# A gated-decay attention, Sinkhorn MoE and bilinear kernel: expert 0 and the gate's logits by 512 tokens, and a first list planned with DMA issue

## The chip, the cores and the metric

One core of one Trainium2 chip. The metric is the device time in microseconds of one execution; the lower the better. PE is TensorE, DVE is VectorE, ACT is ScalarE, POOL is GpSimd, SP is SyncE, which here issues most of the DMAs.

## What is computed

Three layers over 4 x 768 = 3072 tokens, all float32:

```
state = f[t,:,None] * state + k[t] (x) v[t]; y[t] = q[t] @ state     # 4 batches, 8 heads of 48; f = sigmoid(f_logit)
P = exp(y @ w_gate - max); 8 rounds: rows to sum 1, columns to sum 1, times N/E    # 8 experts
x2 = sum over e of P[:, e] * (relu(y @ w1[e]) @ w2[e])              # 384 -> 1024 -> 384
out = ((x2 @ w_a) * (x2 @ w_b)) @ w_out                             # 384 -> 1536 -> 384
```

Products run in a reduced format: every operand is split into a high and a low part, and each product is three matmuls (high x high, high x low, low x high).

## The kernel before, in words

The kernel adds operations to a `Plan`, each with an engine, a cost, the keys it reads and writes and a priority. A scheduler turns the plan into one order for all engines, and the program is issued in that order: each engine works off its own instructions in it strictly one after the other. There are two plans, so two lists.

**The first list** holds the attention, in 24 steps of 128 tokens (`attention`, L624). A step is a chain: transposes of f, q and k (L654), decay factors on ACT and DVE, four groups of small matmuls with masked copies between them (m0 at L697, m8 at L709, m16 at L741, m32 at L752), a transpose of the keys (L763), the state's update (L782), y (L810, L816), and six small DMAs that put y into a tile `xf` with 384 features over partitions. Each buffer of a step exists twice, so two steps are under way at a time, and step s + 2 reuses the buffers of step s: its `q3` (L701) waits until the DMAs of step s have read it.

Beside it, as filler for PE, the first list computes most of expert 0 (`expert0`, L862): x of a block of `EB` = 256 tokens times w1, seven tiles of 128 hidden units with nine matmuls of 256 columns each (L516, the *front*), relu and the split of h on ACT and POOL (L875, L878, L880), then h times w2 (the *down* product). Tokens 0 to 1023 take the down product with tokens over partitions, 384 columns a matmul (L528); blocks in `TURNED` groups (tokens 1024 to 3071) take it with features over partitions, 256 columns a matmul (L539). There are 12 blocks; blocks 0 to 9 and the front of block 10 are in the first list, the down product of block 10 and block 11 in the second. The gate's logits are made per step: six matmuls with x as the stationary side and 16 or 8 columns (`logits`, L854), and a reduce on DVE. Before the first block has its x, PE is kept running by spare matmuls that compute nothing (L917; the plan holds 400, and the list takes as many as fit before the first filler).

The order of the first list comes from `Plan.order` (L132): it keeps a time for each engine, fixed gaps between engines and one delay `LATE` for a DMA; a filler is preferred on PE while a running balance `due`, fed by `SHARE` of the attention's PE time, is not negative. Weights of expert 0 are loaded into two `raw` tiles (`add_piece`, L494) and split into high and low on ACT and POOL (L484, L486) as soon as they land.

**The second list** starts with what is left of expert 0 and the last logits, then the Sinkhorn rounds (`sinkhorn`, L929; each round is one small matmul, L966, between two groups of DVE operations), and then seven experts and the bilinear layer in jobs: a front of 15 products of three matmuls with 512 columns (L1258), whose sums of products run over ACT and DVE (L1539), and backs of 384 or 512 columns (L528, L539). Its first five x pairs `xs` and the weights of its first two jobs (`w1t`) are made ready in the first list (`x_take`, `w1_load`, `w1_split`). Its order comes from `Plan.timed` (L239), which runs `Plan.listed` (L270) 60 times with changed priorities and keeps the best; `listed` already reckons with DMA issue, queue and lanes.

## Time and profile before

| | us |
|---|---|
| runs, lowest / median / highest of 3 | 2155.32 / 2157.52 / 2165.69 |
| the profiled execution's own time | 2153.39 |
| its span, first to last instruction | 2151.6 |
| PE busy (99% of the span) | 2134.3 |
| DVE / POOL / ACT busy | 1720.0 / 1184.4 / 940.9 |

A busy time of PE counts matmuls whose modelled ends overlap the next one's start; the cost of a matmul in a stream is therefore read below from the start of one row to the start of the next. The first list's PE work runs from 0 to about 414 us of the span, the second list from there to the end.

### The profile page before, as it was taken

To read this page: it belongs to the slowest core of one execution; us is meant where nothing else is said; L and a number is where in the kernel's file an instruction comes from. 1 tells how busy PE (TensorE), PEld (TensorE's weight loads), DVE (VectorE), ACT (ScalarE), POOL (GpSimd) and SP (SyncE) were. 2 spreads that over 40 slices of the span, in tenths; PEclk is the share of its full clock that TensorE was granted. 3 is DMA by queue.
4 is the path that set the end of the run, shared out by engine and by line. 5 is a ranking of instruction groups with operands and counts; after the bars stand their busy time and mean duration, and the time that the engine had idled before them with its cause. 6 is when DMAs were issued, how large, how long until landed. Compare 5 with 4: busy or idle time off the path is not lost.

```text
span 2151.6 us, 41006 instructions
## 1 busy us (share of the span) xinstructions
PE 2134.3 (99%) x15371; PEld 1869.3 (87%) x15371; DVE 1720.0 (80%) x2882; ACT 940.9 (44%) x1761; POOL 1184.4 (55%) x1106
## 2 busy tenths in 40 slices
PE   8999999999999999999999999999999999999999
PEld 8999999989989999988888888888888888888888
DVE  7878888377878777698888986899998887866656
ACT  3544454454444445444444444444343445533331
POOL 2212121268877666477787767755545688535322
PEclk9999999999999999999999999999999999999999
DMA  6546644356675567865657678777665766878552
GB/s 133 116 106 165 166 112 98 109 203 241 235 254 196 185 223 267 279 227 194 219 179 232 198 273 279 243 255 247 226 199 174 239 218 228 302 232 283 172 173 74
DMA packets 340951, 438.66 MB, mean 204 GB/s; under 512 B 148024, under 2 KB 224656, under 8 KB 337296
## 3 DMA queue, kind: packets, MB, share of 16 engines
q1 hardware_dynamic: 326016, 422.40, 60.9%
q10 hardware_dynamic: 14736, 13.64, 1.9%
q8 instruction: 121, 1.98, 0.4%
q14 instruction: 78, 0.64, 0.1%
HBM read 295.58 MB, written 135.64 MB: 200 GB/s over the span
## 4 chain that ended last, share of the span: by engine, by line
PE 96%; DVE 3%; DMA 1%; issue 0%; ACT 0%; SPq 0%; DVEq 0%
PE pG L1258 28%; PE pR L539 21%; PE pR L528 18%; PE pF L1258 10%; PE pM L516 4%; PE pM L539 2%; PE pT L654 1%; PE pM L528 1%; PE pA L697 1%; PE pM L917 1%; PE pO L810 1%; PE pA L709 1%; PE pA L741 1%; PE pO L816 1%; PE pO L782 1%; DVE z L1539 1%
## 5 line engine op out<-in xcount | busy, mean ns | idle before, releaser
L539 PE MATMUL pR<-er 128*128 128x512 f32 (+1 forms) x2178 | 537.8, 383 | 0.0
L1258 PE MATMUL pG<-xs,w 128*128 128x512 f32 x1701 | 469.0, 392 | 3.6 <-DVE z L1539 3.0
L539 PEld LDWEIGHTS pR<-er 128*128 128x128 f32 x2178 | 401.1, 188 | 80.5
L528 PE MATMUL pR<-er 128*128 128x384 f32 x2232 | 433.8, 336 | 0.0
L1539 ACT ACTIVATE z<-pG 128x512 f32<-128x512 f32 x397 | 237.2, 598 | 437.5 <-PE pG L1258 370.5
L528 PEld LDWEIGHTS pR<-er 128*128 128x128 f32 x2232 | 397.6, 188 | 23.9
L1258 PEld LDWEIGHTS pG<-xs,w 128*128 128x128 f32 x1701 | 315.9, 188 | 64.3 <-DVE z L1539 3.2
L1539 POOL TENSOR_TENSOR er<-z,er 128x512 fp32r<-128x512 f32 x177 | 246.5, 1400 | 195.9 <-ACT er L1539 135.2
L1539 POOL TENSOR_TENSOR acc<-acc,tmp 128x512 f32<-128x512 f32 x168 | 232.4, 1390 | 173.3 <-DVE tmp L1539 172.3
L1539 ACT ACTIVATE er<-z 128x512 fp32r<-128x512 f32 x353 | 217.6, 628 | 212.4 <-PE pR L539 123.8
L1258 PE MATMUL pG<-er,w 128*128 128x512 f32 x972 | 276.5, 393 | 2.8 <-DVE z L1539 2.6
L1539 DVE TENSOR_TENSOR z<-pF,z 128x512 f32<-128x512 f32 x268 | 182.2, 684 | 64.4 <-PE pF L1258 42.8
L880 POOL TENSOR_TENSOR er<-l,er 128x256 fp32r<-128x256 f32 x84 | 74.6, 891 | 282.3 <-ACT l L878 234.5
L1258 PEld LDWEIGHTS pG<-er,w 128*128 128x128 f32 x972 | 180.9, 188 | 36.5 <-DVE z L1539 4.7
L1539 DVE TENSOR_TENSOR z<-z,pG 128x512 f32<-128x512 f32 x206 | 140.4, 682 | 63.5 <-PE pG L1258 61.9
L1539 POOL TENSOR_TENSOR stage<-stage 128x128 f32<-128x128 f32 x325 | 168.7, 551 | 19.8 <-DMA stage<-in_moe_w_dram 18.2
L1539 DVE SCALAR_TENSOR_TENSOR er<-z,er 128x512 fp32r<-128x512 f32 x150 | 146.6, 986 | 7.4 <-ACT er L1539 7.1
L1539 DVE SCALAR_TENSOR_TENSOR acc<-pR,prob,acc 128x384 f32<-128x384 f32 x168 | 100.5, 611 | 63.0 <-PE pR L528 60.6
L486 POOL TENSOR_TENSOR er<-raw,er 128x384 fp32r<-128x384 f32 (+1 forms) x82 | 94.4, 1159 | 101.8 <-ACT er L484 96.8
L1539 POOL TENSOR_TENSOR w<-stage,w 128x512 fp32r<-128x512 f32 (+2 forms) x75 | 125.0, 1677 | 38.4 <-ACT w L1539 33.5
L1258 PE MATMUL pF<-er,w 128*128 128x512 f32 x486 | 138.8, 394 | 0.0
L1258 PE MATMUL pF<-xs,w 128*128 128x512 f32 x486 | 136.8, 391 | 0.0
(283 smaller groups left out, 3227.0 us busy)
## 6 DMA issues: line engine op xcount, KB each, us to landing
er<-w2d SPq DMA_DIRECT2D x138, 384.0 KB, 4.4
wfmoe<-w SPq DMA_DIRECT2D x19, 1920.0 KB, 7.2
w<-wfmoe SPq DMA_DIRECT2D x38, 768.0 KB, 5.3
w2d<-er SPq DMA_DIRECT2D x69, 384.0 KB, 4.2
w<-wfmoe SPq DMA_DIRECT2D x38, 640.0 KB, 5.6
w<-wfmoe SPq DMA_DIRECT2D x38, 512.0 KB, 4.8
wfout<-w SPq DMA_DIRECT2D x8, 1920.0 KB, 7.7
raw<-in_moe_w_dram SPq DMA_DIRECT2D x64, 192.0 KB, 2.6
```

The lines of the kernel that those rows point to most:

```text
L486: plan.add(prio + 1, "POOL", S_COST[0] + m * S_COST[1], [gk, key], [key], lambda: nc.gpsimd.tensor_tensor(out=lj, in0=got, in1=f32(hj), op ...
L516: nc.tensor.matmul(out=ps, lhsT=a[:, kk, fs], rhs=b[:, kk, :], start=(i == 0), stop=(i == 3 * KD - 1),)
L528: nc.tensor.matmul(out=ps, lhsT=a[:, off:off + 128], rhs=b, start=(start and i == 0), stop=(stop and i == n - 1))
L539: nc.tensor.matmul(out=ps, lhsT=a[:, d * 128:d * 128 + 128], rhs=b, start=(start and i == 0), stop=(stop and i == n - 1))
L654: nc.tensor.transpose(ps[0:R, p * 128:p * 128 + 128], src[:, p * 128:p * 128 + R], ident)
L697: nc.tensor.matmul(out=A0[o:o + 64, w, :], lhsT=pct(bk)[r, g, :], rhs=pct(bq)[r, g, :])
L709: nc.tensor.matmul(out=A1[o:o + 56, 0, w, :].rearrange("j (b e) -> j b e", e=8), lhsT=pct(k3)[r, g, 0:56], rhs=qv[r, g, :, 1, :])
L741: nc.tensor.matmul(out=A1[o:o + 48, 1, w, :].rearrange("j (b e) -> j b e", e=16), lhsT=pct(k3)[r, g, 0:48], rhs=qv[r, g, :, 1, :])
L782: nc.tensor.matmul(out=ps[64 * hd:64 * hd + m, p * D:(p + 1) * D], lhsT=kn[64 * c:64 * c + 64, p * R + 64 * hd:p * R + 64 * hd + m], rhs=b ...
L880: op(POOL, .76, [f"hh{ft}", kf], [f"hl{ft}"], lambda hh=hh, hl=hl, hf=hf: nc.gpsimd.tensor_tensor(out=hl, in0=hf, in1=f32(hh), op=ALU.subt ...
L1258: nc.tensor.matmul(out=ps, lhsT=a[:, slot], rhs=b, start=(new and i == 0), stop=(i == 2), skip_group_check=not new)
L1539: fn()
```

## The change

Expert 0 goes by eight blocks instead of 12 (`E0_BLOCKS`): four of 256 tokens (tokens 0 to 1023, as before) and four of 512 (tokens 1024 to 3071), whose fronts are tiles of nine matmuls with 512 columns and whose down products have 512 columns too. The wide blocks need room: x of blocks 4 and 6 lies in the first three `xs` pairs of the second list, the low part of h in the `w1t` tile of its second job. So the x pairs 0 to 2 can be made only after block 6's front, and the second job's weights are now loaded and split at the start of the second list, behind block 7. Blocks 0 to 5 and the front of block 6 are in the first list; the down product of block 6 and all of block 7 (three times 63 matmuls of 512 columns) in the second.

The logits of blocks 0 to 6 are made turned (`logits_turned`): the gate's weights are the stationary side, 256 or 512 tokens the columns, six matmuls a block; ACT copies the 16 rows out and one transpose for each 128 tokens brings them back. Block 7 keeps the old way. Pieces of expert 0's weights go through five staging tiles instead of two, and their splits wait for a key of attention (`W_AFTER`): the first for the first masked copy of step 0, the others for the x of steps 0 and 1.

The first list now comes from `Plan.first`, a timed list with ranks: costs fitted to this stage (`FIRST`), the shared port of DVE and POOL (operations marked `DVE+`, which many of attention's now are), a cost of changing between attention and filler on PE (`turn`), SP's time to issue each DMA, eight DMAs under way and one queue for their transfers. `SHARE` is 0.3 instead of 0.6. The second list starts from the times at which the first leaves each engine (`late`).

```diff
+    def first(self, share, sooner):
...
+        while any(todo.values()):
+            at, eng = min((max(free.get(eng, 0.0), min(held(n) for n in ns)), eng) for eng, ns in todo.items() if ns)
...
+            turn = due >= 0.0
+            n = min((n for n in todo[eng] if held(n) <= at + 1e-9), key=lambda n: (eng == "PE" and self.ops[n][6] != turn, prio[n]))
...
+            _, _, cost, _, _, late, fill = self.ops[n]
+            cost = self.FIRST[eng].get(round(cost, 3), cost)
+            other = held_by.get(eng) if ready[n] < free.get(eng, 0.0) - 1e-6 else None
+            if n in self.shared and port - .03 > at:
+                at, other = port - .03, on_port
+            if eng == "PE":
+                at = max(at, free[eng] + self.turn(kind, last, self.kind[n]))
+                kind, last, ever = self.kind[n], cost, ever or fill
+                due = max(min(due + (-cost if fill else share * cost), self.MOST), -self.DEBT)
+            count, each = sizes[n]
+            end = at
+            for i in range(count):
+                end = max(end, lanes[landed % self.LANES]) + cost / count
+                queue = max(end + 1.9, queue) + each
+                lanes[landed % self.LANES] = queue + .06
+                landed += 1
+            cost = end - at if count else cost
...
-    SHARE = 0.6
-    LATE = 4.0
-    S_COST, X_COST = (.1, .0026), .9
+    SHARE = 0.3
+    LATE = 2.5
...
+    E0_BLOCKS = [(256, "p"), (256, "q"), (256, "p"), (256, "q"), (512, "r"), (512, "pq"), (512, "r"), (512, "pq")]
+    E0_LEFT = 1.5
+    LG_OLD = 7
+    W1_ON = "DVE"
+    MANY = 2
+    W_BY, W_READS, WG_AFTER = "SP", [], "bk0"
+    W_AFTER = ["X0"], ["st0"], ["st1"]
...
+    ring_of = raw_of + stage_of
...
-        x = count["raw"] % len(raws)
+        x = count["raw"] % len(ring_of)
         count["raw"] += 1
-        raw, rk = raws[x][:, :m], f"raw{x}"
...
+        plan.add(prio, by, cost * len(parts) if by == "SP" else 1.17, reads, rk, get, late)
+        split_ops(plan, prio + 9, raw, [*rk, *after], hj, lj, key, m)
...
+    x_p = er_take(2 * KD * HALF)
+    h_p = er_take(2 * NF0 * HALF)
...
+    x_q = er_take(2 * KD * HALF)
+    x_r = x_all[:, 0:3].rearrange("p a b -> p (a b)")
+    w_r = w1t[1].rearrange("p a b c -> p (a b c)")
...
+    def h_of(b, ft):
+        n = e0_blocks[b][1]
+        lo = area("w", n * ft, n) if n == TB else area("h", n * (NF0 + ft), n)
+        return area("h", n * ft, n), lo
...
+    def logits_turned(plan, b, prio, nm, bufs):
+
+        t0, n, _ = e0_blocks[b]
+        (xH, kH), (xL, kL) = x_tiles(b)
+        m, rk, rt = n // 128, f"raw{b % 2}", raws[b % 2]
+        kl, psl = take(nm, bufs)
+        for i, (x, keys) in enumerate(((xH, kH), (xL, kL))):
+            def lg(i=i, x=x):
+                for kk in range(KD):
+                    nc.tensor.matmul(out=psl[0:2 * E, :n], lhsT=wgs[:, kk], rhs=x[:, kk], start=(i == kk == 0), stop=(i == 1 and kk == KD - 1))
+
+            plan.add(prio, PE, .681 if n == TB else .36, [*keys, *holds(b, True), "wgs"], [kl], lg, kind=5)
+        plan.add(prio, ACT, .6 if n == TB else .37, [kl], [rk], lambda: nc.scalar.activation(
+            out=rt[0:2 * E, :n], in_=psl[0:2 * E, :n], func=AF.Copy))
+
+        def turn():
+            for j in range(m):
+                nc.tensor.transpose(psl[:, 2 * E * j:2 * E * (j + 1)], rt[0:2 * E, 128 * j:128 * j + 128], ident[0:2 * E, 0:2 * E])
+
+        plan.add(prio, PE, .06 * m, [rk], [kl], turn)
+        plan.add(prio, DVE, .16, [kl], [f"lg{t0 // 128 + j}" for j in range(m)], lambda: nc.vector.tensor_reduce(
+            out=logit[:, t0 // 128:t0 // 128 + m, :], in_=psl[:, :2 * E * m].rearrange("p (s two e) -> p s e two", two=2, e=E),
+            axis=AX.X, op=ALU.add))
...
+            for kk in [None]:
+                op(PE, 2.04 if n == TB else 1.08, [*kH, *kL, *holds(b, True), *(wi if kk is None else wi[kk:kk + 1])], [km, "E0i"],
+                   partial(gemm_f, psm[:, :n], w_e0[ft // FT][0], ft % FT, (xH, xL), kk), 0.0, fill)
+            big = n == TB
+            op(ACT, .6 if big else .37, [km], kh, partial(nc.scalar.activation, out=hh, in_=psm[:, :n], func=AF.Relu))
+            hf, kf = b_l[0][:, :n], "l0"
+            op(ACT, .6 if big else .37, [km], [kf], partial(nc.scalar.activation, out=hf, in_=psm[:, :n], func=AF.Relu))
+            op(POOL, 1.29 if big else .76, [*kh, kf], kl, partial(
+                nc.gpsimd.tensor_tensor, out=hl, in0=hf, in1=f32(hh), op=ALU.subtract))
...
+        many = MANY if turned and n == TB else 2
+        for d in range(KD if turned else n // 128):
+            km, psm = take(nm, bufs)
+            cost = .53 if not turned else .681 if n == TB else .36
+            to = psm[:, :n if turned else DM]
+            for f0 in range(0, NF0, many):
+                fs = slice(f0, min(f0 + many, NF0))
+                op(PE, cost * (fs.stop - f0), [k for x in hk[fs] for k in x] + wk[fs] + holds(b), [km, "E0o"], partial(
+                    gemm_d if turned else gemm_t, to, hs[fs], ws[fs], d if turned else d * 128, f0 == 0, fs.stop == NF0), 0.0, fill)
...
+    def e0_weights(u, outs, after):
...
     for i in range(NSTEP):
+        if i == 0 and not W_AFTER[0]:
+            e0_weights(0, False, [])
         attention(i)
+        if i == 0 and W_AFTER[0]:
+            e0_weights(0, False, W_AFTER[0])
+        if i == 1:
+            for u, outs, after in ((1, False, W_AFTER[1]), (0, True, W_AFTER[2]), (1, True, W_AFTER[2])):
+                e0_weights(u, outs, after)
         if i == 0:
...
-        if i:
-            logits(plan, i - 1, 1000 * i + 500, "O", p_O)
-        if i % 2 == 1 and i + 1 < NSTEP:
-            expert0(plan, i // 2, 1000 * (i + 1), "M", p_M, True, 0 if i + 3 > NSTEP - 1 else None)
+        if i and block_of[i - 1] >= LG_OLD:
+            logits(plan, i - 1, 1000 * i + 500, "O", p_O, True)
+        b = block_of[i]
+        if b < LG_OLD and block_of[i + 1] != b:
+            logits_turned(plan, b, 1000 * (i + 1), "O", p_O)
+        if b < len(e0_blocks) - E0_LEFT and block_of[min(i + 1, NSTEP - 1)] != b:
+            expert0(plan, b, 1000 * (i + 1), "M", p_M, True, 0 if b + 1 > len(e0_blocks) - E0_LEFT else None)
...
-    for n in range(2):
+    for n in range(1 if e0_blocks[-1][1] == TB else 2):
         w1_load(plan, 1000 * (15 + 3 * n), n, [f"st{14 + 3 * n}"])
         w1_split(plan, 1000 * (15 + 3 * n) + 600, n, DVE)
     with tc.manual_schedule():
-        for fn in plan.order(SHARE):
+        plan.ranks()
+        for fn in plan.timed(partial(plan.first, SHARE), 1, 0):
             fn()
...
-    plan.add(-9000, "clock", 8.0, [], [f"x{(NSTEP - 1) % 4}"], lambda: None)
-    expert0(plan, NSTEP // 2 - 2, -8000, "R", p_R[:2], False, 1)
+    plan.add(-9000, "clock", max(x_at, 0.0), [], x_of(NSTEP - 1)[1], lambda: None)
+    left = len(e0_blocks) - E0_LEFT
+    for x, b in enumerate(b for b in range(len(e0_blocks) - 1) if b + 1 > left):
+        expert0(plan, b, -8000 + 700 * x, "R", p_R[:2], False, 1 if b < left else None)
     logits(plan, NSTEP - 1, -4000, "R", p_R[:2])
-    expert0(plan, NSTEP // 2 - 1, E0_AT, "R", p_R[:2], False)
+    expert0(plan, len(e0_blocks) - 1, E0_AT, "R", p_R[:2], False)
     guard += ["E0i", "E0o", f"lg{NSTEP - 1}"]
+    if e0_blocks[-1][1] == TB:
+        w1_load(plan, -2000, 1)
+        w1_split(plan, -1000, 1, W1_ON)
...
-        for fn in plan.timed(.08, 0.0, 60, 200):
+        for fn in plan.timed(partial(plan.listed, .08, 0.0), 60, 200):
```

How the order changes on the engines. Over both programs the first list's PE order holds 693 front matmuls of 256 columns, 378 down of 256 and 168 of 384 before, in 136 stretches (66, 46 and 24) between other work; in the change 252 front of 256, 168 down of 384, 189 front and 126 down of 512, in 90 stretches (22, 28, 18 and 22). Spare matmuls fall from 193 to 185, and the 48 transposes, three m0 and so on that precede the first filler are the same.

PE in the first list, a place in a block of tokens from 1024 on; before (`pM` is expert 0's bank, `pA` and `pT` attention's; m16 is the 48x32 group, m32 the 32x32 one):

```order
L539 MATMUL pM_167<-er 128x256 x12
L516 MATMUL pM_166<-er 128x256 x9
L752 MATMUL pA_165<-q_137,k_139 32x32 x16
L539 MATMUL pM_167<-er 128x256 x3
L654 MATMUL pT_160<-ident,nat_f_117 112x128 x4
L697 MATMUL pA_164<-bq_132,bk_134 64x64 x16
L763 MATMUL pO_162<-ident,k_139 128x112 x4
L516 MATMUL pM_167<-er 128x256 x9
```

And in the change (L642 is the front, L869, L901, L857 and L912 are m8, m16, m0 and m32):

```order
L869 MATMUL pA_161<-q_132,k_134 56x32 x16
L642 MATMUL pM_163<-xs,er 128x512 x9
L901 MATMUL pA_161<-q_132,k_134 48x32 x16
L857 MATMUL pA_160<-bq_129,bk_131 64x64 x16
L814 MATMUL pT_157<-ident,nat_f_112 112x128 x4
L814 MATMUL pT_156<-ident,nat_q_114 112x128 x4
L642 MATMUL pM_162<-xs,er 128x512 x9
L912 MATMUL pA_161<-q_132,k_134 32x32 x16
```

A filler tile now stands for twice the columns, there are fewer of them, and attention's groups stand closer together.

PE at the start of the second list, among the Sinkhorn rounds (L966, then L1146, is the matmul of one round; `pG` and `pF` are banks of the experts' fronts); before:

```order
L516 MATMUL pR_6603<-er 128x256 x9
L516 MATMUL pR_6604<-er 128x256 x9
L966 MATMUL pR_6605<-prob,share 128x200
L516 MATMUL pR_6603<-er 128x256 x9
L1258 MATMUL pG_6598<-xs_78,w_79 128x512 x3
L516 MATMUL pR_6604<-er 128x256 x9
L1258 MATMUL pG_6598<-xs_6624,w_79 128x512 x3
L966 MATMUL pR_6605<-prob,share 128x200
```

And in the change:

```order
L642 MATMUL pR_5890<-er 128x512 x9
L642 MATMUL pR_5891<-er 128x512 x9
L1146 MATMUL pR_5892<-prob,share 128x200
L642 MATMUL pR_5890<-er 128x512 x9
L642 MATMUL pR_5891<-er 128x512 x9
L1146 MATMUL pR_5892<-prob,share 128x200
L642 MATMUL pR_5890<-er 128x512 x9
L642 MATMUL pR_5891<-er 128x512 x9
```

Expert 0's wide matmuls now fill the rounds; 27 matmuls of the experts' fronts stand between the last logits and the two transposes that end the rounds (L1157), and 33 follow these in a row.

DVE at the start of the program (`fi` holds decay factors, the two numbers of a name are steps 0 and 1); before:

```order
L661 TENSOR_SCALAR fi_128<-e_130 112x512
L661 TENSOR_SCALAR fi_129<-e_131 112x512
L669 TENSOR_TENSOR fi_128<-e_130,fi_128 112x512
L671 SCALAR_TENSOR_TENSOR fi_128<-fi_128,e_130 112x512
L669 TENSOR_TENSOR fi_129<-e_131,fi_129 112x512
L677 TENSOR_TENSOR fi_128<-fi_128 112x128x2
```

And in the change:

```order
L821 TENSOR_SCALAR fi_124<-e_126 112x512
L829 TENSOR_TENSOR fi_124<-e_126,fi_124 112x512
L831 SCALAR_TENSOR_TENSOR fi_124<-fi_124,e_126 112x512
L837 TENSOR_TENSOR fi_124<-fi_124 112x128x2 x3
L843 TENSOR_TENSOR bq_128<-pT_157,fi_124 112x64x3
L843 TENSOR_TENSOR bk_130<-pT_156,fi_124 112x64x3
```

Step 0 goes ahead of step 1 instead of in turns with it.

## Rows read from the trace of the kernel before

**Rows 1.** Cores: span and mean granted clock.

```profile
core 0: 2151.6 us, clock 0.999
```

**Rows 2.** Windows: stretch, length, busy us per engine (instructions), PEclk, DMA share, GB/s.

```profile
20.00:55.00 35.00, 33.31 (x698) 30.92 (x695) 30.63 (x73) 13.36 (x28) 7.92 (x7) 1.00 0.55 119
55.00:409.30 354.30, 352.46 (x6346) 328.86 (x6345) 285.56 (x694) 169.75 (x417) 70.67 (x77) 1.00 0.51 120
...
422.50:470.00 47.50, 44.02 (x253) 38.08 (x252) 33.45 (x74) 26.19 (x55) 25.55 (x31) 0.96 0.50 178
```

**Rows 3.** Timeline of PE, first list: start, length, line, operation, count.

```profile
162.81 1.33 PE L516 MATMUL pM<-er 128*128 128x256 f32 x9
164.07 0.91 PE L741 MATMUL pA<-q,k 48*48 48x32 f32 x32
...
176.24 1.33 PE L516 MATMUL pM<-er 128*128 128x256 f32 x9
177.50 0.32 PE L810 MATMUL pO<-X,Y 64*48 64x64 f32 x4
...
198.70 0.83 PE L854 MATMUL pO<-wgs,er 128*128 128x16 f32 x6
199.39 0.77 PE L528 MATMUL pM<-er 128*128 128x384 f32 x3
```

**Rows 4.** Timeline of PE, end of the first list: a long run of 256 columns.

```profile
409.27 5.65 PE L516 MATMUL pM<-er 128*128 128x256 f32 x45
414.76 7.89 PE L539 MATMUL pR<-er 128*128 128x256 f32 x63
```

**Rows 5.** Timeline of PE, second list: a run of 512 columns.

```profile
1002.81 2.20 PE L539 MATMUL pR<-er 128*128 128x512 f32 x9
1004.85 1.52 PE L1258 MATMUL pG<-xs,w 128*128 128x512 f32 x6
```

**Rows 6.** Timeline of PE, start of the program.

```profile
9.82 8.64 PE L917 MATMUL pM<-er 128*128 128x256 f32 x70
19.10 0.62 PE L654 MATMUL pT<-ident,nat_k 128*112 128x128 f32 x4 [0.65 <-issue]
...
21.91 1.02 PE L709 MATMUL pA<-q,k 48*56 48x32 f32 x32 [0.53 <-DVE q L701]
...
35.11 0.77 PE L741 MATMUL pA<-q,k 48*48 48x32 f32 x26 [1.00 <-DVE k L722]
...
55.17 2.32 PE L516 MATMUL pM<-er 128*128 128x256 f32 x18
```

**Rows 7.** Timeline of PE, the Sinkhorn rounds.

```profile
458.86 1.65 PE L1258 MATMUL pG<-er,w 128*128 128x512 f32 x3 [2.61 <-DVE z L1539]
...
463.98 0.93 PE L1258 MATMUL pG<-xs,w 128*128 128x512 f32 x3 [0.87 <-DVE z L1539]
```

**Rows 8.** Windows, the same place; columns as in rows 2.

```profile
458.90:462.00 3.10, 3.10 (x8) 2.62 (x9) 2.84 (x8) 1.35 (x3) 0.44 (x1) 0.50 1.03 431
```

**Rows 9.** Timeline of PE: m0 of steps 1, 3, 4, 6 and 23.

```profile
25.54 1.13 PE L697 MATMUL pM<-bq,bk 48*64 48x64 f32 x32
...
59.45 1.08 PE L697 MATMUL pA<-bq,bk 48*64 48x64 f32 x29
...
76.33 1.11 PE L697 MATMUL pA<-bq,bk 48*64 48x64 f32 x31
...
103.36 1.15 PE L697 MATMUL pA<-bq,bk 48*64 48x64 f32 x32
...
383.54 1.15 PE L697 MATMUL pA<-bq,bk 48*64 48x64 f32 x32
```

**Rows 10.** Page, groups: count | busy us, mean ns | idle before.

```profile
L1539 POOL TENSOR_TENSOR er<-z,er 128x512 fp32r<-128x512 f32 x177 | 246.5, 1400 | 195.9 <-ACT er L1539 135.2
...
L880 POOL TENSOR_TENSOR er<-l,er 128x256 fp32r<-128x256 f32 x84 | 74.6, 891 | 282.3 <-ACT l L878 234.5
```

**Rows 11.** One line on DVE, 55 to 409.3 us: count, min/median/max ns.

```profile
L720 DVE TENSOR_TENSOR q<-q,g x42: 406/425/1199, 63.8 to 396.9; 112x256 f32<-112x256 f32 x42
```

More of the change, by code (lines that the diff above doesn't have):

```diff
@@ new lines, with sizes @@
+    COUNT = {"SP": {1.16: 2, 4.2: 6, 2.41: 3, 2.4: 4, 1.2: 2}, "ACT": {2.2: 3, 1.17: 2}}
+    SMALL = .0009
+    def sizes(self, n):
+        _, eng, cost, _, _, late, _ = self.ops[n]
+        key, cost = self.key.get(n, ""), round(cost, 3)
+        count = self.COUNT[eng].get(cost, 1) if eng == "SP" or (eng == "ACT" and late > 0) else 0
+        size, pieces = {"na": (196e3, 1024), "vn": (196e3, 1024), "wg": (4e3, 64), "xd": (196e3, 384), "xg": (96e3, 192)}.get(key[:2], (256e3, 128))
+        if key[:1] == "Y":
+            size, pieces = 49e3, 256
+        if key[:2] == "xf" and count > 1:
+            size, pieces = 32e3 * count, 64 * count
+        return count, (size / self.DMA_RATE + pieces * self.SMALL) / max(count, 1)
@@ L237, with timed @@
     PAUSE, BACK, STEPS = .25, 40.0, 60
-    def timed(self, near, far, passes, by):
+    def timed(self, lister, passes, by):
         sooner, best = {}, None
         for _ in range(passes):
-            made, span, waits = self.listed(near, far, sooner)
+            made, span, waits = lister(sooner)
             if best is None or span < best[0]:
-                best = (span, made)
+                best = (span, made, waits)
             for n in self.behind(made, waits):
                 sooner[n] = sooner.get(n, 0) - by
+        self.ends = {self.ops[n][1]: best[2][n][1] for n in best[1]}
+        self.when = best[2]
         return [self.ops[n][4] for n in best[1]]
@@ L282, in listed @@
                 todo[o[1]].append(n)
-        free, port, queue, run, now, made = dict.fromkeys(self.ENGINES, 0.0), 0.0, 0.0, 0.0, 0, []
+        free = {eng: max(self.late.get(eng, 0.0), 0.0) for eng in self.ENGINES}
+        port, queue, run, now, made = 0.0, 0.0, 0.0, 0, []
         width, place, paused = 0, 0, False
@@ L426 @@
            for nm, n in (("m1", 1), ("m2", 1), ("mb", 1), ("r", NTILE), ("c", E))}
[L427 removed]
+    x_all = big.tile([128, NXA, 2 * TB], F32R, name="xs")
+    xpair = [x_all[:, n].rearrange("p (two t) -> p two t", two=2) for n in range(NXA)]
     w1t = [big.tile([128, 2, NW, 128], F32R, name=f"w1{n}") for n in range(2)]
@@ L595 @@
     PE, DVE, ACT, POOL, SP = "PE", "DVE", "ACT", "POOL", "SP"
-    plan = Plan(same=.1, over=.07, ranked=True, early=2000, slack=.8)
+    plan = Plan(port=True)
     used = {"T": 0, "O": 0, "M": 0}
@@ L915 @@
-    for n in range(2):
-        nc.vector.tensor_copy(out=b_hh[0][:, 128 * n:128 * n + 128], in_=ones)
-    plan.spare(PE, .11, 400, lambda: nc.tensor.matmul(
-        out=p_M[1][:, :EB], lhsT=b_hh[0][:, 0:128], rhs=b_hh[0], start=True, stop=True))
-    for u in range(2):
-        (ih, il), (oh, ol) = w_e0[u]
-        rows = moe_rows(0, u * FU, 128 * e0_f[u])
-        for n in range(KD):
-            add_piece(plan, 1000 + 120 * (7 * u + n), f"e0i{u}{n}", rows[n], ih[:, n], il[:, n])
-        for n in range(e0_f[u]):
-            f0 = u * FU + n * 128
-            add_piece(plan, 1000 + 120 * (7 * u + KD + n), f"e0o{u}{n}", [(0, 128, w2[0, f0:f0 + 128, :])],
-                      oh[:, n], ol[:, n])
+            plan.add(prio, *a, kind=5 * (fill and a[0] == PE))
@@ new lines @@
+    for n in range(2):
+        nc.vector.tensor_copy(out=h_p[:, 128 * n:128 * n + 128], in_=ones)
+    plan.spare(PE, .11, 400, lambda: nc.tensor.matmul(
+        out=p_M[1][:, :HALF], lhsT=h_p[:, 0:128], rhs=h_p[:, 0:HALF], start=True, stop=True))
+    def e0_weights(u, outs, after):
+        (ih, il), (oh, ol) = w_e0[u]
+        if outs:
+            for n in range(e0_f[u]):
+                f0 = u * FU + n * 128
+                add_piece(plan, 1000 + 120 * (7 * u + KD + n), f"e0o{u}{n}", [(0, 128, w2[0, f0:f0 + 128, :])],
+                          oh[:, n], ol[:, n], after=after)
+            return
+        for n, row in enumerate(moe_rows(0, u * FU, 128 * e0_f[u])):
+            add_piece(plan, 1000 + 120 * (7 * u + n), f"e0i{u}{n}", row, ih[:, n], il[:, n], W_READS if u == 0 else (), after=after, by=W_BY if u == 0 else "SP")
@@ L1150 @@
     with tc.manual_schedule():
-        for fn in plan.order(SHARE):
+        plan.ranks()
+        for fn in plan.timed(partial(plan.first, SHARE), 1, 0):
             fn()
     a_ctx.close()
+    late = {eng: at - plan.ends["PE"] for eng, at in plan.ends.items()}
+    x_at = max(plan.when[w][1] for w in (plan.last[k][0] for k in x_of(NSTEP - 1)[1])) - plan.ends["PE"]
     sbb = ctx.enter_context(tc.tile_pool(name="sbb", bufs=1, reuse_waits="tile"))
```

313 lines of the change are left out of this document (186 added, 127 removed).

## The prediction

> **What bounds the kernel now.** The first view is that of the cores: a span of 2151.6 us at a granted clock of 0.999 [rows 1], so the clock is no loss to speak of. The profiled execution took 2153.39 us; the median of the runs, 2157.52, lies 4.1 above it, so I make the sum against the profile and carry the difference over to the median. The second view is the windows [rows 2]: from 55 to 409.3 us, where attention and expert 0 share PE, PE is busy 352.46 of 354.30 us, while DVE is at 81%, ACT at 48% and POOL at 20%. Only between 422.5 and 470 does PE lose time worth naming: 3.5 us idle, at a clock of 0.96. So time is PE's work put end to end, and an edit pays if it takes work from PE or closes one of few holes. What must be asked then is whether a shorter PE leaves another chain standing: DVE at 81% is the next.
>
> **Part by part.** *Columns.* Expert 0 for tokens 1024 to 3071 takes 1008 matmuls of 256 columns before (eight blocks, 63 front and 63 down each) and 504 of 512 in the change. In an unbroken run 45 of 256 columns take 414.76 - 409.27 = 5.49 us, 122 ns each [rows 4]; nine of 512 take 2.04 us, 227 ns each [rows 5]. 123.0 against 114.3 us: **-8.7**. No row shows 512 columns in the first list; the nearest other value is that 512 cost just twice 256, a gain of nothing, which is one end.
>
> The Trainium skill bears on this place ("TensorE: Matmul & The Clock Gate", Back-to-back issue gap): there a warm matmul takes columns / 2.4 GHz plus 2.5 ns, and by an estimate from it widening would save 504 x 2.5 ns = 1.3 us instead of 8.7. The rows disagree: what 256 and 512 columns take lies some 15 and 13 ns above the columns' own time, so I go by the rows.
>
> *Stretches.* Nine matmuls between attention's small groups take more than in a run: six such tiles start between 162.81 and 176.24 and take 1.26, 1.26, 1.18, 1.15, 1.24 and 1.26 us (first and last shown) [rows 3], mean 1.225 against 9 x 0.122 = 1.098, so each stretch costs 0.127. The order has 136 stretches before and 90 after: 46 x 0.127 = **-5.8**.
>
> *Logits.* A tile costs 199.39 - 198.70 = 0.69 us [rows 3]; 20 of 24 tiles go turned, -13.8. In their place stand four times six matmuls of 256 columns (2.9), three times six of 512 (4.1), 20 transposes at about the 0.115 of one old logits matmul, an estimate (2.3), and 14 stretches at 0.127 (1.8): +11.1. Net **-2.7**. ACT's seven copies lie on an engine at 48%.
>
> *Start.* Eight spare matmuls fewer, at (19.10 - 0.65 - 9.82)/70 = 0.123 us [rows 6], make -1.0. Before the first filler at 55.17 PE waits 0.65, 0.53 and 1.00 us, 2.2 in all [rows 6]. In the change step 0 goes ahead of step 1 on DVE and the weights' splits on POOL come later; but where its list waits instead, no row tells. From all 2.2 saved to 2 more than before, I take half: together **-2.1**.
>
> *Moved work.* The second list's 189 leftover matmuls grow from 23.1 to 42.8 us; those 19.8 leave the first list. For PE that is zero in sum, since both lists are one queue. It is the cover that changes. In the second list these matmuls fill the Sinkhorn rounds, where PE waited 2.61 and 0.87 us for DVE [rows 7] and, after the first of these, ran 3.1 us at half clock (0.50: the lower of the two levels, 1.2 GHz) [rows 8], a loss of 1.55: 5.0 in all. All of it can go; against that stands the second job's weight split, which now starts behind block 7, and 33 front matmuls in a row afterwards whose sums wait for DVE. From -5.0 to +5.0, I take half of the gain, **-2.5**.
>
> *New waits in the first list.* From the first filler to the last attention, PE now loses 19.8 + 8.7 + 5.8 + 2.7 us of work, and 4.7 more because the filler behind the last attention grows (45 x 0.122 to 45 x 0.227): 41.7 of 354.1. m0 of step 3 starts at 59.45 and of step 23 at 383.54 [rows 9]: 16.2 us a step, which must become 16.2 x (1 - 41.7/354.1) = 14.3. DVE's work stays near 285.56 us, so its share goes from 81% to 91%. At 88% (30.63 of 35.00) between 20 and 55 us [rows 2] PE waited 0.53 and 1.00 us for DVE, 4.4%; over 312 us that is 14. That is the upper end, for there no filler was at hand; the lower is none. I take **+5**, nearer to none.
>
> The sum: -8.7 - 5.8 - 2.7 - 2.1 - 2.5 + 5 = -16.8, so 2136.6 against the profile and **2141** against the median.
>
> **The rivals.** *Rival 1, the attention's chain, ends slower.* Step s + 2 needs step s's buffers, so two steps' chains set a floor to the pace. It decides from here: without new waits the sum is -21.8 at 14.3 us a step, and each us of pace adds 20, so the gain is gone at 15.4, and if the chain holds the old 16.2 while the second list still pays the 19.8, it is +16: 2174. For it: from m0 of step 1 to that of step 3, 25.54 to 59.45, with little but spare matmuls on PE, 33.9 us passed, 17.0 a step [rows 9]; a filler tile now holds attention's next matmul for 2.0 instead of 1.1 us, and a POOL split takes 1400 ns at 512 columns against 891 at 256 [rows 10], beside DVE operations that take 406 ns at least and up to 1199 [rows 11]. Against it: steps 4 to 6, 76.33 to 103.36, ran at 13.5 a step with full fillers [rows 9], and the start was slowed by an order that took the two steps in turns. A middle case at 15.4, with the gain just gone, ends at 2157.
>
> The Trainium skill ("SBUF — State Buffer", section "SBUF: two separate sides") says that DVE operations with two SBUF inputs and GpSimd operations take turns on a shared port pair, held for a whole instruction. Rows 11 agree in kind; by that rule a longer POOL split makes the longest hold longer, and fewer of them (49 instead of 77) hold less in sum.
>
> *Rival 2: columns cost the same in either width*, as the page above would nearly have it. Then -8.7 falls away: 2149. Only the row of 512 columns speaks against it, and that lies in another list.
>
> *Rival 3: the start of the second list gets worse.* The sums of 33 fronts queue on DVE and PE waits there once more as much as before: +5.0 instead of -2.5, 2148. For it: PE waited there for just such sums [rows 7]. Against: the 33 follow the last round, when DVE has nothing of Sinkhorn left.
>
> **How the numbers follow.** Forecast 0.62, rival 1 in full 0.09 and in its middle case 0.12, rival 2 0.07, rival 3 0.10. A difference of 0.5% (10.8 us) is about what a measurement of this kernel tells from no change; the bound is 2146.7. Below it lie the forecast but for 0.02 and half of rivals 2 and 3: 0.68. Above 2168.3 lies rival 1 in full and a little more, 0.10. The rest is 0.22. The good ends of all terms make -8.7 - 5.8 - 2.7 - 3.2 - 5.0 = -25.4, 2128 against the profile, which is the low end. With the bad ends of start, seam and waits (+1, +5, +14) the sum is about +3, 2160: the high end, which leaves out rival 1 in full and a little below.
>
> **What would show it.** Columns: rows of nine matmuls of 512 columns in the first list some 2.1 to 2.2 us apart. Stretches and pace: m0 to m0 at about 14.6 us a step, DVE near 90%. Logits: seven groups instead of 20. Start: the first filler between 51 and 55 us. Seam: no half clock, waits of PE under 2.5 us in sum up to the last round. The first list's last matmul should fall near 381 us. Wrong it is if PE's waits in the first list exceed 15 us (rival 1), if nine wide matmuls take 2.45 us (rival 2), or if PE waits over 5 us behind the rounds (rival 3).

## The result, and the profile after

The change takes 2140.18 us (median of 4 runs, 2137.25 to 2141.49) against 2157.2 for the kernel before: a ratio of 0.9912, 95% interval 0.9883 to 0.994. A second measurement (e9 below) gave 0.9910 (0.9895 to 0.9925). The forecast was 2141, faster by over 0.5%. The sum was right, by errors that cancelled: several of its terms were not.

The profiled execution took 2137.25 us. Cores, then windows of the kernel after (columns as in [rows 2]):

```profile
core 0: 2135.4 us, clock 0.999
```

```profile
20.00:52.80 32.80, 29.48 (x574) 27.62 (x573) 29.32 (x62) 15.20 (x33) 15.12 (x11) 1.00 0.73 166
52.87:382.04 329.17, 326.46 (x5833) 282.95 (x5832) 273.50 (x662) 162.35 (x357) 53.63 (x50) 0.99 0.53 123
52.87:373.75 320.88, 318.17 (x5798) 276.11 (x5796) 271.79 (x659) 157.47 (x348) 49.09 (x46) 0.99 0.54 125
396.90:436.20 39.30, 38.91 (x175) 31.55 (x174) 28.93 (x74) 17.85 (x33) 13.88 (x10) 1.00 0.27 97
51.00:53.20 2.20, 1.41 (x38) 1.37 (x39) 2.20 (x5) 0.00 (x0) 0.45 (x1) 0.99 0.86 160
53.20:56.50 3.30, 3.30 (x18) 3.23 (x17) 2.00 (x8) 1.68 (x6) 0.73 (x1) 0.50 0.88 168
```

The shared stretch lasts 329 us with the filler behind the last attention (second line). Without it (third line), as [rows 2] has it, it lasts 321 us where 354 were needed. PE is again busy but for 2.7 us, and DVE is at 85% in the third line, with 271.79 us of work where it had 285.56. The fourth line is the place of the Sinkhorn rounds: no half clock (0.50 in [rows 8]) and 0.4 us idle. But the last line shows a new loss: behind a wait before the first filler, PE runs 3.3 us at 0.50, 1.2 GHz, which costs 1.65.

Timeline of PE after, the start and the pace (m0 is L857, m32 L912):

```profile
1.64 2.71 PE L1095 MATMUL pM<-er 128*128 128x256 f32 x11 [1.64 <-DVE er L1094]
...
46.73 0.91 PE L901 MATMUL pA<-q,k 48*48 48x32 f32 x32 [0.80 <-DVE k L882]
47.57 1.69 PE L1095 MATMUL pM<-er 128*128 128x256 f32 x12
51.79 0.69 PE L912 MATMUL pA<-q,k 48*32 48x32 f32 x32 [2.52 <-DVE k L882]
...
52.87 3.79 PE L642 MATMUL pM<-er 128*128 128x256 f32 x18
...
58.77 1.15 PE L857 MATMUL pA<-bq,bk 48*64 48x64 f32 x32
...
347.29 1.15 PE L857 MATMUL pA<-bq,bk 48*64 48x64 f32 x32
```

The first filler starts at 52.87 (55.17 in [rows 6]); m0 of step 3 to m0 of step 23 is 288.5 us, 14.4 a step (16.2 in [rows 9]). The same view, wide tiles in the first list and its end:

```profile
241.21 2.32 PE L642 MATMUL pM<-xs,er 128*128 128x512 f32 x9
243.46 0.94 PE L942 MATMUL pO<-vn,kn 64*64 64x48 f32 x32
244.33 2.35 PE L642 MATMUL pM<-xs,er 128*128 128x512 f32 x9
246.61 0.32 PE L970 MATMUL pO<-X,Y 64*48 64x64 f32 x4
...
373.75 8.46 PE L642 MATMUL pM<-xs,er 128*128 128x512 f32 x36
382.04 0.39 PE L664 MATMUL pR<-er 128*128 128x512 f32 x1
```

A lone wide tile, one between attention's groups, takes 2.25 and 2.28 us here (mean of 16 such: 2.240), not 9 x 0.227 = 2.04. The list's longest run of wide matmuls takes 8.29 us for 36, 0.230 each, and the list ends at 382.04. In the rounds (L1146 is the round's matmul) PE goes from one filler to the next without a bracket:

```profile
404.50 0.50 PE L1146 MATMUL pR<-prob,share 128*128 128x200 f32 x2
404.70 4.41 PE L642 MATMUL pR<-er 128*128 128x512 f32 x18
408.95 0.51 PE L1146 MATMUL pR<-prob,share 128*128 128x200 f32 x2
...
436.17 0.48 PE L1157 MATMUL pR<-ident,prob 128*117 128x128 f32 x2 [0.39 <-DVE prob L1142]
...
442.82 0.96 PE L1451 MATMUL pG<-xs,w 128*128 128x512 f32 x3 [0.69 <-ACT pc L1737]
```

PE's whole time can be split by kind of work if each timeline row counts from its start to the next row's, less the idle time in the next row's brackets. That gives this account (us), by which the experiments are read too; "rest" is all of the second list that is not expert 0:

| | before | after | e1 narrow | e5 narrow, filled |
|---|---|---|---|---|
| up to the first filler | 55.17 | 52.87 | 51.50 | 54.96 |
| first list from there: attention's groups | 165.87 | 167.71 | 168.16 | 168.94 |
| expert 0 | 177.19 | 147.76 | 177.73 | 163.20 |
| logits | 14.72 | 11.16 | 11.30 | 12.60 |
| waits | 1.81 | 2.54 | 5.52 | 5.83 |
| second list: expert 0 | 23.16 | 44.16 | 22.78 | 38.18 |
| rest | 1713.7 | 1709.2 | 1718.8 | 1709.2 |
| span | 2151.6 | 2135.4 | 2155.8 | 2152.9 |

### The profile page after: what moved, and what is told of

The parts are those of the page before. It is cut to its first block, busy times and chain, and to the rows that moved or that the text cites. A ratio compares the mean times of both kernels' runs of the same rounds, so it can differ in the third digit from the quotient of the medians.

```text
span 2135.4 us, 39656 instructions
## 1 busy us (share of the span) xinstructions
PE 2119.3 (99%) x14801; PEld 1827.0 (86%) x14801; DVE 1729.8 (81%) x2869; ACT 939.4 (44%) x1700; POOL 1177.6 (55%) x1078
## 4 chain that ended last, share of the span: by engine, by line
PE 92%; DVE 5%; DMA 1%; ACT 1%; issue 1%; ACTq 0%; SPq 0%; DVEq 0%
PE pG L1451 28%; PE pR L664 22%; PE pR L653 18%; PE pF L1451 10%; PE pM L642 3%; PE pT L814 1%; PE pM L664 1%; PE pM L653 1%; DVE z L1737 1%; PE pA L857 1%; PE pO L970 1%; PE pA L869 1%; PE pO L976 1%; PE pR L642 1%; PE pA L901 1%; PE pO L942 1%
## 5 line engine op out<-in xcount | busy, mean ns | idle before, releaser
L664 PE MATMUL pR<-er 128*128 128x512 f32 x2136 | 548.8, 389 | 0.0
L1737 POOL TENSOR_TENSOR stage<-stage 128x128 f32<-128x128 f32 x325 | 167.1, 545 | 17.2 <-DMA stage<-in_moe_w_dram 14.7
L1737 DVE SCALAR_TENSOR_TENSOR er<-z,er 128x512 fp32r<-128x512 f32 x150 | 152.9, 1023 | 11.7 <-ACT er L1737 9.3
L1737 DVE TENSOR_TENSOR z<-pG,z 128x512 f32<-128x512 f32 x145 | 99.6, 687 | 47.4 <-PE pG L1451 45.2
L613 POOL TENSOR_TENSOR er<-raw,er 128x384 fp32r<-128x384 f32 (+1 forms) x75 | 86.2, 1156 | 66.5 <-ACT er L611 63.4
```

The source lines that it names most:

```text
L613: plan.add(prio + 1, "POOL", S_COST[0] + m * S_COST[1], [*gk, key], [key], lambda: nc.gpsimd.tensor_tensor(out=lj, in0=got, in1=f32(hj), o ...
L664: nc.tensor.matmul(out=ps, lhsT=a[:, d * 128:d * 128 + 128], rhs=b, start=(start and i == 0), stop=(stop and i == n - 1))
L1737: fn()
```

## The experiments

**e1: narrow blocks,** with the planner, the turned logits and the order of expert 0's weights of the change. With a narrow last block the second job's weights are loaded and split in the first list again, and no x pair has to wait for block 6.

```diff
-    E0_BLOCKS = [(256, "p"), (256, "q"), (256, "p"), (256, "q"), (512, "r"), (512, "pq"), (512, "r"), (512, "pq")]
-    LG_OLD = 7
+    E0_BLOCKS = [(256, "p"), (256, "q")] * 6
+    LG_OLD = 11
```

> The change with all 12 blocks of expert 0 at 256 tokens, so 45 fewer wide columns nowhere: 1008 matmuls of 256 columns instead of 504 of 512; planner, turned logits, weights' order stay. Theory A (the prediction's terms): columns 8.7 and stretches are lost, and with 23.1 instead of 44 us of leftover in the second list the holes among the Sinkhorn rounds come back (2.5 to 5.0 us): 2152 to 2157. Theory B (rows of the trace after: expert 0 in all is worth 8.4 us, not 14.5): 2149 plus what the holes bring, 2149 to 2153. Theory C (the new planner alone made the gain): 2140, no different from the change.

2156.93 us, ratio 1.0008 (0.9998 to 1.0018): the whole gain is gone. Theory C falls. Expert 0 takes 200.5 us in the two lists against 191.9 in the change and 200.35 before, though e1 has 122 stretches in the first list, 14 fewer than before. So the wide blocks are worth 8.6 us there, with all that they bring along. The second list's rest is 9.6 us longer than in the change. PE's waits at e1's rounds, then its window there:

```profile
458.36 0.96 PE L1451 MATMUL pG<-er,w 128*128 128x512 f32 x3 [1.40 <-DVE z L1737]
460.76 1.62 PE L1451 MATMUL pG<-xs,w 128*128 128x512 f32 x3 [1.44 <-DVE z L1737]
```

```profile
452.00:470.00 18.00, 15.00 (x65) 11.68 (x64) 14.44 (x27) 10.12 (x20) 10.26 (x11) 0.81 0.62 212
```

The holes of [rows 7] are back, and a mean clock of 0.81 over 18 us costs 18 x 0.19 = 3.4 us more. Why e1's rest is also 5.1 us longer than that of the kernel before, with as much cover, stays open.

Timeline of e1, m0 of steps 3 and 23 and the end of the first list:

```profile
56.60 1.15 PE L857 MATMUL pA<-bq,bk 48*64 48x64 f32 x32
...
352.11 1.15 PE L857 MATMUL pA<-bq,bk 48*64 48x64 f32 x32
...
386.19 1.69 PE L664 MATMUL pM<-er 128*128 128x256 f32 x12
...
414.21 1.96 PE L664 MATMUL pR<-er 128*128 128x256 f32 x15
```

Attention runs at 14.8 us a step here with the narrow tiles, and ends at 386.19; what it left of expert 0 follows until 414.21 (414.76 before). So the time from m0 to m0 follows how the order mixes attention with fillers, and not only how much work PE has.

**e5: narrow, but with twice the cover in the rounds.** Against e1, 126 more narrow matmuls (block 9's down product and block 10's front) are left to the second list, and blocks 10 and 11 are issued behind the last logits; block 10's logits go the old way. The main lines, against e1:

```diff
-    E0_LEFT = 1.5
-    LG_OLD = 11
+    E0_LEFT = 2.5
+    LG_OLD = 10
...
-    expert0(plan, len(e0_blocks) - 1, E0_AT, "R", p_R[:2], False)
+    expert0(plan, len(e0_blocks) - 2, E0_AT - 3000, "R", p_R[:2], False)
+    expert0(plan, len(e0_blocks) - 1, E0_AT - 1500, "R", p_R[:2], False)
```

> As e1_narrow (expert 0 at 256 tokens throughout, 2156.93 us), but with block 10's front and down product also left to the second list and placed among the Sinkhorn rounds, so that narrow matmuls of expert 0 cover them for twice as long (30.8 us in place of 15.4). Theory A (the seam's gain comes from cover alone): of the 9.6 us that e1's second list is longer than that of the change, the two waits of 1.4 us and most of the rest go; 2148 to 2152, the rest of the distance to 2140 is columns (8.6 us). Theory B (the gain comes from the later load of the second job's weights, or from wide tiles): 2155 to 2158, no change.

2152.59 us, ratio 0.999 (0.998 to 1.0001), against e1's 1.0008: some 4 us less, by intervals that just overlap, and just above theory A's range. Windows of e5, the rounds and behind them:

```profile
405.50:450.00 44.50, 44.50 (x315) 41.80 (x315) 24.83 (x64) 19.40 (x45) 14.63 (x26) 1.00 0.18 63
450.00:470.00 20.00, 20.00 (x132) 18.57 (x132) 13.32 (x17) 14.82 (x34) 14.12 (x12) 1.00 0.77 274
```

PE is busy throughout at full clock, and the rest falls from 1718.8 to 1709.2, the change's. So cover alone, without the wide tiles and the later weights, closes the seam. (e5's start is 3.5 us later than e1's; 1.5 of it is a matter of the execution, see the end.)

**e2: old logits throughout.**

```diff
-    LG_OLD = 7
+    LG_OLD = 0
```

> The change with the old logits for all 24 tiles (six matmuls of 16 or 8 columns for each 128 tokens). By the prediction's term the turned logits are worth 2.7 us: 2143. By the rows of the trace after, where 7 turned groups and 3 old tiles take 11.2 us against 15.4 before, 4.2 us: 2144.4. Rival: they are hidden in what the order does with them, and nothing changes: 2140.

2146.38 us, ratio 0.9952 (0.9938 to 0.9967): about 9 us slower than the change by the ratios, not 4, and the rival falls. The logits up to the end of the first list take 15.75 against 11.16, 4.6 us, as the rows said. The other half is not theirs: the order comes out otherwise, PE waits 7.6 us there (longest 3.1 for L847), and the clock falls behind it (window of e2):

```profile
50.00:100.00 50.00, 45.94 (x877) 42.55 (x875) 43.12 (x99) 22.85 (x53) 13.06 (x13) 0.90 0.51 110
```

**e3: the old rule of order for the first list,** with the new blocks. The old rule's gaps are set and the shared port is left out, but the rule works with the change's delays and costs. For `xf` it reckons with 1.45 us where the kernel before had 4.5. The change's costs for DVE are lower than the old ones, and e3 takes another 0.07 us off: `q` times `g` stands at 0.25 us, where the kernel before had 0.42 and [rows 11] show 0.425. So this is not the order that the old rule would have made with its own numbers. The main lines:

```diff
+        plan.ranked, plan.early, plan.slack, plan.same, plan.shared = True, 2000, .8, .1, set()
+        plan.ops = [(p, g, c - (.07 if g in ("DVE", "ACT") else 0.0), *o) for p, g, c, *o in given]
+        made = plan.order(.6)
...
-        for fn in plan.timed(partial(plan.first, SHARE), 1, 0):
+        plan.timed(partial(plan.first, SHARE), 1, 0)
+        for fn in made:
             fn()
```

> The change with the first list ordered by the old rule (balance with share 0.6, ranks, no DMA lanes, no shared port), all else as in the change. Theory A: the planner is worth the start's 2.3 us alone, 2142. Theory B: it is what kept PE's waits in the first list at 2.5 us where the prediction had feared 5 to 14 more: with the old order waits of 5 to 14 us come back and the time is 2145 to 2154. Theory C: the first list follows the wide tiles whatever the order, 2140.

2214.72 us, ratio 1.0272 (1.0255 to 1.0289), far beyond all three. Theory C falls. Theory B has the right place, but 37 us of waits where it had 5 to 14, and over 70 us of time. PE's waits in the first list of e3 (who waits, for whom, us in total, times, longest) and two of its windows:

```profile
PE pA L912 <- DVE k L882: 10.6, 6, 2.9
PE pA L901 <- DVE k L882: 6.6, 6, 2.2
PE pT L814 <- ACT bq L847: 4.4, 3, 3.2
```

```profile
200.00:300.00 100.00, 92.14 (x1493) 76.46 (x1495) 71.19 (x169) 38.99 (x81) 9.58 (x7) 0.90 0.54 137
350.00:400.00 50.00, 42.86 (x683) 35.68 (x679) 36.47 (x92) 17.13 (x36) 1.25 (x1) 0.83 0.30 71
```

36.9 us of waits stand in the first list (2.5 in the change), and attention's groups take 194.9 instead of 167.7 us, because the clock falls behind the waits. The pace is 17.6 us a step, with DVE at 71 to 73%. So attention's chain does bind once its operations come in a bad order, with DVE far from full. What the old rule would lose with its own costs and delays, and with it what the new planner is worth beside the wide tiles, is not shown.

**e6: more moved out of the first list.**

```diff
-    E0_LEFT = 1.5
+    E0_LEFT = 2.5
```

> The change with E0_LEFT = 2.5: the down product of block 5 and the front of block 6 (126 matmuls of 512 columns, 28.6 us) leave the first list too, whose pace must become 14.4 - 28.6/20 = 13.0 us a step. Theory A (attention's chain has room): PE's waits in the first list stay under 4 us and the time within 2 us of the change, 2138 to 2142. Theory B (rival 1's floor, which e3_old_order showed at 17 us a step with another order, lies between 13 and 14.4 us): PE waits 10 to 30 us more there, with half clock behind the waits: 2150 to 2170.

Here x pairs 0 to 2 are made over block 6's x before its front reads it, so that block's part of the output comes from other data; the instructions are the same. 2162.72 us, ratio 1.0041 (1.0027 to 1.0055). Theory B: m0 of step 23 starts at 347.24, as in the change (347.29), 14.35 us a step, and not earlier. The list ends only 12.8 us earlier for 28.6 us less work. Windows of e6, then of the change:

```profile
300.00:350.00 50.00, 44.49 (x885) 37.70 (x880) 44.42 (x103) 23.74 (x50) 8.72 (x6) 0.94 0.47 115
350.00:400.00 50.00, 46.39 (x413) 39.81 (x413) 18.36 (x43) 18.57 (x34) 8.03 (x6) 0.78 0.56 187
```

```profile
300.00:350.00 50.00, 49.78 (x873) 41.37 (x867) 44.50 (x102) 23.03 (x48) 8.34 (x6) 1.00 0.52 135
350.00:400.00 50.00, 49.88 (x498) 40.85 (x496) 18.45 (x35) 22.55 (x42) 10.29 (x8) 1.00 0.43 136
```

Where the fillers are missing PE idles and then runs at a lower clock. So from 300 us to m0 of step 23 attention's chain sets the time under this order, and less work for PE gains nothing there. It is no floor for every order: e4's, below, runs at 14.2 us a step.

**e7: wide down products in one piece.**

```diff
-    MANY = 2
+    MANY = 7
```

> The change with a wide down product of all 7 tiles as one piece of 21 matmuls instead of pieces of 6: 10 stretches of them in place of 29, and 85 instead of 101 stretches of expert 0 in all up to the rounds. Theory A (the prediction's 0.127 us for each stretch): -2.0, 2138. Theory B (each wide stretch costs 0.19, rows of the trace after): -3, 2137. Theory C (e1_narrow against before: 14 stretches fewer at the same 200.4 us of expert 0, so a stretch has no price of its own): no gain, and pieces of 4.8 us hold attention's next matmul, 2140 to 2146.

2153.55 us, ratio 0.9998 (0.999 to 1.0007): 15.8 us more than the change by the spans of the two profiles (2151.2 against 2135.4), and more than theory C gave. The expert 0 part did get 2.75 us cheaper for 13 stretches fewer in the first list (145.0 against 147.8), as theories A and B wanted, but 1.5 dearer in the second. Attention's pace goes from 14.4 to 15.3 us, the list ends at 388.98, and PE waits at its end, with fewer fillers left (window of e7):

```profile
375.00:389.00 14.00, 10.86 (x225) 9.91 (x219) 8.11 (x17) 6.59 (x13) 1.27 (x1) 0.73 0.25 68
```

Of the 15.8 us, 3.0 lie ahead of the first filler (1.5 of them PE's first wait, see the end), 3.9 in the first list and 8.9 in the second, where waits of 2.3 us for `prob` return in the rounds (L1146). One piece of 4.8 us can be seen to hold attention up: `k` (L882) is ready at 322.80, but m16 (L901) starts at 326.12, behind the piece that began at 321.12.

```profile
322.39 0.41 DVE L882 TENSOR_TENSOR k<-k,g 112x256 f32<-112x256 f32 x1
```

```profile
321.12 0.51 PE L664 MATMUL pM<-er 128*128 128x512 f32 x1
...
326.12 0.91 PE L901 MATMUL pA<-q,k 48*48 48x32 f32 x32
```

How much of the 15.8 us such holds make is not shown: the second list has longer pieces too.

**e4, e8 to e12: the wait before the first filler.** e4 makes spare matmuls cheaper for the planner, so that more are taken; e8 makes the low part of expert 0's weights on DVE; e9 is the change again, e10 is e8 again, e11 is e4 and e8 together, e12 is e8 with down products in pieces of 3 matmuls (`MANY = 1` for 2).

```diff
-                    cost = .215 if free[eng] < 8.0 else .12
+                    cost = .215 if free[eng] < 8.0 else .1
```

```diff
-        plan.add(prio + 1, "POOL", S_COST[0] + m * S_COST[1], [*gk, key], [key], lambda: nc.gpsimd.tensor_tensor(
+        plan.add(prio + 1, "DVE+", .1 + m * .0012, [*gk, key], [key], lambda: nc.vector.tensor_tensor(
```

```diff
-    MANY = 2
+    MANY = 1
```

> The change with the planner's price of a spare matmul at 0.10 instead of 0.12 us, so that 218 instead of 185 spares stand before the first filler. It tests the half clock that follows PE's wait of 2.52 us at 51.79 us in the trace after (0.50 for about 3.4 us, 1.7 us lost). Theory A: spares fill that wait, the clock stays at 1.00 from 52 to 58, and 1.7 us are gained: 2138.5. Theory B: the additional spares (33 at 0.14, 4.6 us) stand ahead of attention's own matmuls and delay its chain, so the first filler comes later by up to 4.6 us: 2141 to 2145.

> The change with the low parts of expert 0's weights made on DVE instead of POOL (13 pieces, at 0.55 us some 7 us more for DVE). In the trace after, seven POOL splits run from 35 to 51.5 us while operations of DVE that take 0.41 us alone take 1.21 to 1.23, and PE waits 2.52 us at 51.79. Theory A (POOL's operations hold DVE longer than DVE's own would): that wait and the half clock behind it go, 2 to 4 us are gained, 2136 to 2138. Theory B (DVE, busy 89% from 20 to 53 us, is the bound there): the first filler comes 2 to 4 us later, 2142 to 2146.

> The change itself, for a comparison on the chip of the next three. It also shows whether PE's first wait (1.64 us here, 3.13 in the profile of before, and 3.14 in e5 to e8, whose lists begin alike) belongs to the kernel: if it is 3.14 in some execution of this same kernel, 1.5 us of the start's gain is not the change's. Expected: 0.991 to 0.993 of before, 2.52 us of wait before m32 of step 2, half clock behind it.

> e8_split_on_dve again, beside the change on one chip. Theory A (the wait before m32 and the half clock behind it were worth 2 to 4 us): 0.998 to 0.9985 of the change, 2 to 4 us less. Theory B (what the start gains is lost later in the first list, where the first filler is earlier but the end not as much): less than 1 us apart.

> The low parts on DVE and the planner's price of a spare at 0.10 us together (216 spares). Theory A: the two gains share one cause, PE's idle time before the first filler and the clock behind it, so that the second adds nothing: 2133 to 2137, as e8. Theory B: they add up: 2131 to 2133.

> The low parts on DVE, and the wide down products in pieces of 3 matmuls (0.68 us) instead of 6: 107 instead of 102 stretches. e7_many_7 held attention up with pieces of 4.8 us and took 16 us more. Theory A (attention's next matmul still waits for pieces of 1.4 us): 1 to 3 us less than e8, 2132 to 2134. Theory B (a stretch costs 0.13 to 0.19 us and attention has no more to gain): 1 us more, 2136.

| | us, median | ratio to before (95%) |
|---|---|---|
| e4 more spares | 2137.56 | 0.9913 (0.9897 to 0.9928) |
| e8 low parts on DVE | 2135.16 | 0.9915 (0.9903 to 0.9927) |
| e9 the change again | 2136.75 | 0.9910 (0.9895 to 0.9925) |
| e10 as e8 | 2134.17 | 0.9894 (0.9880 to 0.9908) |
| e11 both | 2142.82 | 0.9931 (0.9916 to 0.9945) |
| e12 as e8, pieces of 3 | 2135.06 | 0.9899 (0.9886 to 0.9912) |

e9 to e12 ran on one chip and can be compared in us; e4 and e8 ran on two others, where the kernel before took 2155.63 and 2153.92. e4 fills the wait as meant (only PE's first wait is left ahead of its first filler, and no half clock follows), but a wait of 2.9 us for `prob` appears in the rounds, and its ratio is the change's. e10 shows the mechanism on one line, `k` times `g` on DVE up to 60 us (count, min/median/max ns), in the change and in e10:

```profile
L882 DVE TENSOR_TENSOR k<-k,g x6: 414/417/1229, 16.0 to 50.5; 112x256 f32<-112x256 f32 x6
```

```profile
L882 DVE TENSOR_TENSOR k<-k,g x6: 414/417/419, 16.1 to 51.9; 112x256 f32<-112x256 f32 x6
```

With POOL out of the way no such operation takes 1.2 us; a split costs DVE some 0.61 us (L613: 3.6 us for 6 of the 11) and the first filler starts at 45.64 instead of e9's 53.88, with the clock at 1.00 behind it. Yet the first list ends only 5.2 us earlier (376.04 against 381.25): 2.1 us of attention's groups only moved behind the first filler, and PE waits 0.85 us more there. Of this 2.6 us reach the end: 2134.17 against 2136.75, by intervals that overlap a little. e8, the same kernel, has the change's ratio on its chip, so e10 has the lowest median, but a gain over the change is not clear of noise. Theory B of e8 falls, for its first filler comes earlier (46.72); e10's 2.6 us fit the 2 to 4 us of its theory A, no more. Finer pieces (e12) bring nothing more. e11 is 8.7 us worse than e10, against both its theories: its other order waits behind the first fillers, and the clock from 51 to 100 us is 0.90:

```profile
51.00:100.00 49.00, 47.10 (x819) 41.74 (x819) 40.24 (x101) 22.36 (x54) 7.47 (x8) 0.90 0.53 111
```

## Why the prediction was right, and where its terms were not

The terms against the profile, from the account above (-16.2 in all; -16.8 was forecast):

| term | predicted | measured |
|---|---|---|
| columns, at the prices of unbroken runs | -8.7 | -8.6 |
| stretches | -5.8 | -2.7 |
| half clock behind 51.79, and breaks of expert 0 by the rounds | - | +1.7, +1.2 |
| logits | -2.7 | -4.2 |
| start without its logits | -2.1 | -1.6 |
| seam (rest of the second list) | -2.5 | -4.5 |
| waits in the first list | +5 | +0.7 |
| attention's groups there | 0 | +1.8 |

*Columns: right, within 1 or 2 us.* 504 x 0.227 against 1008 x 0.122 is the forecast's own product. By the 0.230 of the longest wide run it would be about -7, and the wide stretches would cost less; only both together are measured. Either way a wide matmul costs less than two narrow ones (0.244), and rival 2 falls. That e1's 8.6 us equal the term is partly chance: against e1 the change also saves 3.3 us of stretches (below: 14.7 instead of 18.0) and loses about as much by the half clock and the breaks in the rounds. The estimate from the Trainium skill ("TensorE: Matmul & The Clock Gate", Back-to-back issue gap) was 1.3 us; the measurement decides against it here. The section gives that formula for a single matmul, and says that in a stream the weight loads set the spacing as well.

*Stretches: mis-sized.* The step took 0.127 us for each of 90. Before, expert 0's 177.19 us less 1071 x 0.122 and 168 x 0.173 leave 17.4 us for 136 stretches, 0.128 each. After, 147.76 less 252 x 0.122, 315 x 0.227, the same 168 and 1.65 of half clock leave 14.7 for 90: 0.164. The 0.173 is a run of 384 columns after, 2.60 us for 15:

```profile
457.53 2.77 PE L653 MATMUL pR<-er 128*128 128x384 f32 x15
460.13 0.86 PE L1451 MATMUL pG<-xs,w 128*128 128x512 f32 x3
```

A lone wide tile costs 2.240 - 2.04 = 0.20 us above its columns (0.17 at 0.230 each), a lone narrow one before 1.225 - 1.098 = 0.13 (mean of 53). So a break in a stream of 512 columns costs more here, and fewer breaks save half of what was counted. In e1, 14 fewer breaks saved nothing (18.0 us against 17.4). What sets the price is open.

*Logits: right in kind, too small.* Of the 4.2 us, 3.6 lie behind the first filler and 0.7 ahead of it. The stretches that I charged to them (1.8) don't show.

*Start: right by luck.* Of -1.6, 1.5 is the first wait of PE, 1.64 instead of 3.13 us, and that is not the kernel's (last section). The waits behind it rose from 2.2 to 3.75 us, where I had taken half of 2.2 away. The moved splits did what rows 10 and 11 had warned of: the late ones meet, POOL works from 45.4 to 51.5 us almost without a pause, operations of DVE triple in length (L882: 0.42 to 1.21 and 1.23 us), PE waits 2.52 us and the clock falls. The half clock that the change takes from the seam comes back there. The Trainium skill ("SBUF — State Buffer", SBUF: two separate sides) tells of the shared port held for a whole instruction; the 1229 ns that become 419 in e10 agree.

*Seam: right, and most of the 5.0 rather than half.* What I held against it, 33 fronts in a row, costs 0.69 and 0.19 us of waits, behind 0.39 for the last round. Rival 3 falls; e5 shows that cover is the cause. But the size moves from one execution to another: in e9, the change again, the rest is 1710.8 instead of 1709.2, with waits of 0.83 and 0.71 us for `prob`, and the gain 2.9 instead of 4.5.

*Waits and rival 1: the right danger, the wrong condition.* I had the waits grow with DVE's share, and DVE's work stay at 285.56 us. It fell to 271.79, mostly because the making of the x pairs and the second job's weight split left this stretch; so the share is 85%, not 91, and PE waits 0.7 us more. I also derived the pace of 14.3 from PE's work alone, but e1 runs at 14.8 with as much of expert 0 as before. The pace follows the order too, which I had credited with the start alone. e3 shows how much an order can lose: with the same work the chain holds 17.6, and the time is 2214.72, worse than rival 1's 2174. And e6 shows that little is left: from 300 us to m0 of step 23, less work for PE gains nothing. My reason for +5 was wrong, and so was the margin that I saw.

The sum was thus right by luck, because errors of both signs met. Stretches (3.1 us), half clock and breaks in the rounds (2.9), attention's groups (1.8, of which 0.9 lay ahead of the first filler before) and the start (0.5) came out worse than forecast; logits (1.5), seam (2.0) and waits (4.3) came out better. Of the signs named, lone wide tiles lie 2.16 to 2.28 us apart instead of 2.1 to 2.2, the pace is 14.4 (14.6), DVE 85% (near 90), first filler 52.87 (51 to 55), last matmul 382.04 (381).

## What to carry to other kernels

Widening a matmul pays what a run of either width shows in the trace, but here a break in a wide stream cost more than one in a narrow stream (0.20 against 0.13 us), and a long filler piece can hold a chain up (3.3 us behind a piece of 4.8 us in e7). Take work from PE and the chain beside it becomes the limit (e6); what it can do depends on the order of its operations, not on the busy share of an engine (e3: 74 us more than the change at 72% of DVE). Work that can be placed freely is worth most where a serial stretch, here the Sinkhorn rounds, leaves PE waiting: 9.6 us of the second list from e1 to e5, for cover alone, of which some 4 us reach the whole.
